# Decay attention with queries on partitions: scores, maximum and exponential on one tile, then transposes

## The chip, the cores and the metric

The kernel runs on one core of a Trainium2 chip. The metric is the device time of one execution in microseconds (us), lower is better. A core has five engines with a queue each, worked off in the order in which the program was written: TensorE (PE, matmuls; its loads of the stationary operand are shown apart as PEld), VectorE (DVE), ScalarE (ACT), GpSimd (POOL) and SyncE (SP, which issues most transfers). Engines wait for one another through semaphores.

## The reference

```
scores = scale * np.matmul(q, k.transpose(0, 1, 3, 2))
log_f = np.log(np.clip(f, 0.0001, 1.0))
cum = np.cumsum(log_f, axis=-1)
decay = cum[:, :, :, None] - cum[:, :, None, :]
scores = np.where(causal, -1000000000.0, scores + decay)
scores = scores - np.max(scores, axis=-1, keepdims=True)
attn = np.exp(scores)
attn = attn / (np.sum(attn, axis=-1, keepdims=True) + 1e-09)
x = np.matmul(attn, v)            # then heads side by side: (B * S, H * D)
h = np.maximum(x @ w_in, 0.0)
out = h * h @ w_out
```

There are 8 batches of 8 heads, that is 64 heads, of S = 576 positions and D = 64 channels. The second part, called the MLP below, has 4608 tokens, 512 channels and 2048 hidden units. All data are float32.

## The kernel before, in words

**Two precisions.** The first NWHOLE = 14 heads ("whole" heads) use float32 operands in the matmuls. All later heads and the MLP ("split" work) write each operand as a high part rounded to float32r plus a low part, and add two or three float32r products.

**Attention, keys on partitions.** For a head, `score` (line 382) makes six units. A unit has up to 128 keys on the partitions and the queries that may see them in the free dimension; the six have 320, 320, 192, 64, 448 and 256 columns, 1600 causal columns in all. Since the maximum of a query runs over partitions there, it is computed earlier and apart: `max_units` (336) makes the product a second time with queries on partitions, and a VectorE instruction (353) adds the causal mask and reduces to the maximum. For whole heads `turn_maxima` (370) turns the maxima into a row by five matmuls with an identity matrix (376); for split heads a transfer writes them as a row (358). The row is an extra contraction row of the score product, as are the two rows of the cumulated decay. So the score product has the maximum subtracted already, and ScalarE takes the exponential from PSUM (408). In split heads GpSimd then zeroes the masked triangle (410), ScalarE makes the high part (423) and VectorE the low part (424). `av_part` (438) multiplies by v: one float32 matmul per piece in whole heads (455), three float32r matmuls in split heads (434 to 436: low x high, high x low, high x high). A column of ones in v gives the denominators; `finish` (472) sends them through DRAM to spread them over the partitions and multiplies (491). Head 7 does the same with matmuls (`finish_here`, 495).

**MLP.** Work is cut into 18 chunks of 256 tokens and 16 slices of 128 hidden units. `mlp1` (548) makes 12 matmuls of 256 columns (554), then ScalarE and VectorE make relu, its square and the split of it (562 to 565). `mlp2` (568), one step behind, makes 6 matmuls of 512 columns (577). A call of either is a "half". The weights arrive as 64-bit floats and are converted by `weight_ops` (185), four VectorE instructions, two on ScalarE and one on GpSimd for each of 32 tiles.

**Order.** Every engine follows the order of the program (`in_order`, 768). The loop at line 739 goes through slots, six for each head. In a slot it issues one score unit, the product with v of the unit two slots earlier (`LAG`), and then whatever the table `events` holds: loads, preparation (`prep`, 304), maxima of the next head. `fill` (662) puts MLP halves into each half of a slot, at the rate at which batches become ready; the MLP can start when batch 0 is done, after eight heads. What is left of the MLP when attention is over (three chunks) runs alone at the end.

**PSUM.** There are eight banks of 512 float32 columns; the table `banks` says which are used for scores (s), maxima (m), the product with v (av), `mlp1` (h) and `mlp2` (o0, o1). It changes when the MLP starts.

## Time and profile before

| | |
|---|---|
| three timed runs | 1221.43, 1227.12, 1228.7 us; median 1227.12 |
| the profiled execution | span 1223.8 us from the first to the last instruction; no other time of its own is given |
| PE busy | 1190.8 us (97%) |
| DVE, ACT, POOL busy | 779.6, 711.3, 371.7 us |
| eight heads without MLP | 0 to 106.2 us |
| attention and MLP together | 106.2 to about 1088 us |
| MLP alone | about 1088 to 1223.8 us |

A row of a timeline has the start, the time from there to the modelled end, the engine, the line, the operation, and the tiles as "written <- read". Since matmuls are pipelined, the distance from one start to the next is what a matmul costs its engine; the duration in the row also has the way through the array. A row of the groups has the summed busy time, the mean of one instruction in ns, and the idle time before it. A row of the windows has for each engine the busy time and the number of instructions, and for PE the granted clock, 1.00 being full speed.

### The profile page before, as it was taken

The page shows a single profiled execution, that of the slowest core. Times are in us where ns is not written, and L with a number is a line of the kernel's source. Part 1 is how long each engine was busy: PE and PEld are TensorE (multiplying, and loading weights), DVE is VectorE, ACT ScalarE, POOL GpSimd, SP SyncE. Part 2 cuts the span into 40 slices and gives each one's busy share as a digit, 9 for nine tenths or more (in the row PEclk, how much of TensorE's full clock was granted, in tenths as well). Part 3 has the DMA queues.
Part 4 walks back from the last instruction along what each step waited for, and adds up shares of the span by engine and source line. Part 5 has one row for each costly group of instructions (what it writes and reads, how often), then busy time and mean ns, then how long its engine had stood idle before and what let it go on. Part 6 is the DMA issues. An engine that isn't in the chain of part 4 may idle for free. (4 is left out here: it accounts for less than half of the span.)

```text
span 1223.8 us, 23339 instructions
## 1 busy us (share of the span) xinstructions
PE 1190.8 (97%) x7808; PEld 1049.1 (86%) x7808; DVE 779.6 (64%) x2049; ACT 711.3 (58%) x1748; POOL 371.7 (30%) x565
## 2 busy tenths in 40 slices
PE   6999998999999999999999999999999999999998
PEld 3666886888998899999999989998999899999997
DVE  5779876666766767675655776667676667533332
ACT  2676665656666666665656566666666666533232
POOL 3333324333334333332322333333333333200000
PEclk7989999999999999999999999999999999999999
DMA  8758500221211212111111111212121212000000
GB/s 234 198 149 237 139 26 17 59 59 39 56 42 40 51 42 58 42 34 41 44 32 43 44 42 42 59 41 54 35 51 37 59 42 59 11 28 11 8 18 18
DMA packets 105912, 71.58 MB, mean 58 GB/s; under 512 B 87848, under 2 KB 87848, under 8 KB 105792
## 3 DMA queue, kind: packets, MB, share of 16 engines
q1 hardware_dynamic: 104672, 65.96, 21.3%
q0 software_dynamic: 1120, 4.13, 1.4%
q8 instruction: 62, 1.02, 0.4%
q14 instruction: 58, 0.48, 0.1%
HBM read 59.91 MB, written 9.87 MB: 57 GB/s over the span
## 5 line engine op out<-in xcount | busy, mean ns | idle before, releaser
L577 PE MATMUL bank<-w,gh 128*128 128x512 f32 x1152 | 414.1, 400 | 0.0
L554 PE MATMUL bank<-xh,w 128*128 128x256 f32 x2304 | 328.5, 285 | 0.2 <-DVE xh L541 0.2
L424 DVE TENSOR_TENSOR pl<-p,ph 128x320 fp32r<-128x320 f32 (+4 forms) x300 | 186.7, 622 | 198.2 <-ACT ph L423 192.1
L554 PEld LDWEIGHTS bank<-xh,w 128*128 128x128 f32 x2304 | 300.6, 189 | 7.8 <-ACT r L562 1.2
L577 PEld LDWEIGHTS bank<-w,gh 128*128 128x128 f32 x1152 | 217.6, 189 | 38.2
L562 ACT ACTIVATE r<-bank 128x256 f32<-128x256 f32 x288 | 110.5, 384 | 208.4 <-PE bank L554 175.9
L577 PE MATMUL bank<-w,gl 128*128 128x512 f32 x576 | 227.2, 394 | 0.1
L563 DVE TENSOR_TENSOR g<-r 128x256 f32<-128x256 f32 x288 | 126.2, 438 | 134.9 <-ACT r L562 134.4
L423 ACT CAST ph<-p 128x320 fp32r<-128x320 f32 (+4 forms) x300 | 124.4, 415 | 150.1 <-POOL p L410 107.6
L410 POOL TENSOR_SCALAR_AFFINE_SELECT p<-p 128x128 f32<-128x128 f32 (+1 forms) x250 | 81.2, 325 | 427.9 <-ACT p L408 321.0
L554 PE MATMUL bank<-xl,w 128*128 128x256 f32 x1152 | 184.2, 282 | 0.0
L353 DVE CUSTOM_DVE_ANT_0 bank<-bank,mz 128x256 f32<-128x256 f32 (+4 forms) x320 | 133.9, 432 | 41.3 <-PE bank L345 39.5
L554 PEld LDWEIGHTS bank<-xl,w 128*128 128x128 f32 x1152 | 157.8, 190 | 0.2 <-DVE xl L542 0.2
L408 ACT ACTIVATE p<-bank 128x320 f32<-128x320 f32 (+4 forms) x300 | 116.3, 388 | 64.0 <-PE bank L401 52.8
L565 DVE TENSOR_TENSOR gl<-g,gh 128x256 fp32r<-128x256 f32 x288 | 127.9, 444 | 35.8 <-ACT p L408 1.0
L345 PE MATMUL bank<-rk 66*128 66x320 f32 (+4 forms) x384 | 112.6, 324 | 18.1 <-DMA rk<-qkraw 10.1
L564 ACT ACTIVATE gh<-r 128x256 fp32r<-128x256 f32 x288 | 120.6, 419 | 9.4
L577 PEld LDWEIGHTS bank<-w,gl 128*128 128x128 f32 x576 | 109.3, 190 | 14.3 <-DVE gl L565 0.9
L434 PE MATMUL bank<-pl,vh 128*65 128x320 f32 (+4 forms) x350 | 97.1, 277 | 2.3 <-ACT den L470 2.3
L345 PEld LDWEIGHTS bank<-rk 66*128 66x128 f32 (+1 forms) x384 | 69.2, 187 | 32.9 <-issue 11.9
L435 PE MATMUL bank<-ph,v 128*64 128x320 f32 (+4 forms) x350 | 94.9, 271 | 0.0
L436 PE MATMUL bank<-ph,vh 128*65 128x320 f32 (+4 forms) x350 | 93.6, 273 | 0.0
(92 smaller groups left out, 1539.5 us busy)
## 6 DMA issues: line engine op xcount, KB each, us to landing
qkraw<-in_qk SPq DMA_DIRECT2D x50, 288.0 KB
v<-in_v SPq DMA_DIRECT2D x64, 160.0 KB
out<-osb SPq DMA_DIRECT2D x36, 256.0 KB
den<-rdr SPq DMA_DIRECT2D x62, 144.0 KB
w<-in_w_in SPq DMA_DIRECT2D x16, 512.0 KB
w<-in_w_out SPq DMA_DIRECT2D x16, 512.0 KB
rl<-in_qk SPq DMA_DIRECT2D x14, 288.0 KB
rk<-in_qk POOLq DMA_DIRECT2D x14, 288.0 KB, 5.5
```

The costliest lines, as they stand in the source:

```text
L345: nc.tensor.matmul(ps[:m, :n], st["r2"][:D + 2, q0:q0 + m], st["kl0"][:D + 2, k0:k0 + n], start=True, stop=True,)
L353: nc.vector.tensor_tensor_reduce(out=ps[:m, :n], in0=ps[:m, :n], in1=mz[:m, mo:mo + n], op0=ALU.add, op1=ALU.min, scale=-1.0, scalar=init, ...
L408: nc.scalar.activation(out=p[:kn, :n], in_=ps[:kn, :n], func=AF.Exp, scale=SCALE)
L423: nc.scalar.copy(out=ph[:kn, :n], in_=p[:kn, :n])
L424: nc.vector.tensor_tensor(out=pl[:kn, :n], in0=p[:kn, :n], in1=ph[:kn, :n].bitcast(F32), op=ALU.subtract,)
L434: nc.tensor.matmul(acc[:D + 1, o], vh, pl[:kn, i], start=first, stop=False)
L554: nc.tensor.matmul(ph[:, :T], w[:, s, cc], x[:, cc, :], start=(cc == 0 and k == 0), stop=(cc == NCC - 1 and k == 2),)
L562: nc.scalar.activation(out=r, in_=ph[:, :T], func=AF.Relu)
L563: nc.vector.tensor_tensor(out=g, in0=r, in1=r, op=ALU.mult)
L564: nc.scalar.activation(out=gh, in_=r, func=AF.Square)
L565: nc.vector.tensor_tensor(out=gl, in0=g, in1=gh.bitcast(F32), op=ALU.subtract)
L577: nc.tensor.matmul(po, g[:, ts], w[:, s], start=(fc == 0 and k == 0), stop=(fc == NF - 1 and k == 2),)
```

## The change

**Layout.** Scores are made with the queries on partitions. The queries of a head are five tiles: tile 0 has 64, tiles 1 to 4 have 128, and tile i sees 64, 192, 320, 448 or 576 keys, again 1600 columns. `unit` does one to two tiles: the score matmuls, a VectorE instruction that adds the mask and reduces to the maximum, and the exponential on ScalarE with the maximum as its bias and the denominator as its accumulated output. `max_units`, `turn_maxima`, the mask matmuls (394), the triangle on GpSimd (410), `finish`, `finish_here`, and their transfers go away.

**Scaling.** `normalize` takes the reciprocals of the five denominators (two VectorE instructions) and scales the five tiles in place on GpSimd, widest first.

**Turning.** `turn` makes 15 PE transposes of 128x128 blocks for a head, in four groups that fill PSUM banks C, D, C, D. ScalarE copies each group to SBUF; in split heads this copy is the high part, and VectorE makes the low part from PSUM.

**Product with v.** `attend`, in five parts, uses [v high | v low] as one stationary operand of 128 columns with the high probabilities and v high with the low ones: two matmuls for each piece in place of three. The two halves of the result lie on different partitions; ScalarE copies one and VectorE adds it.

**Rest.** NWHOLE becomes 10. A weight tile's clamp moves from VectorE to GpSimd. Low and high parts of q and k are placed by transfers (`prep`). Scores get PSUM tiles A and B of two banks each; from the start of the MLP on only A, and the product with v only E. There are two sets of probability tiles up to head 10 and one after it. The slots before head 0 are dropped, and weights are converted at a rate of 1.3 steps per slot.

The diff, cut to its core (new functions as they stand in the changed kernel; of the removed lines, which the listing above shows, only a few):

```diff
-    NWHOLE = 14
+    NWHOLE = 10
+    NDOUBLE = 11
-    banks = {"av": [0, 6], "s": [1, 2, 3], "m": [4, 5, 7], "h": [4], "o0": [6], "o1": [7]}
+    banks = {"s": ["A", "B"], "t": ["C", "D"], "av": ["E", "F"], "h": ["F"], "o": ["B"]}
...
+    probs = [[cpool.tile([P, wide(i)], F32, name=f"p{i}") for i in range(NQ)]]
...
-            nc.vector.tensor_scalar(mag, mag, MAG_LOW, MAG_HIGH, ALU.max, ALU.min)
+                nc.gpsimd.tensor_scalar(mag, mag, MAG_LOW, MAG_HIGH, ALU.max, ALU.min)
...
+    def prep(h, part):
+        st = state[h]
+        if part == 0:
+            st["x"] = wk.tile([P, S], F32R, name="qkr", bufs=1)
+            nc.vector.tensor_copy(out=st["x"], in_=st["raw"])
+            st["r"] = Planes(wk.tile([P, 2 * S], F32R, name="rl"))
+        if part == 1:
+            raw = st["raw"]
+            nc.gpsimd.tensor_tensor(out=raw, in0=raw, in1=st["x"].bitcast(F32), op=ALU.subtract)
...
+            nc.sync.dma_start(out=f32(r.q[:D]), in_=f32(x[:D]))
+            nc.sync.dma_start(out=f32(r.k[D:]), in_=f32(x[D:]))
+            nc.sync.dma_start(out=f32(r.q[D:]), in_=y[:D])
+            nc.sync.dma_start(out=f32(r.k[:D]), in_=y[D:])
...
+            load_cum(h, rounded.k)
+            nc.sync.dma_start(out=f32(rounded.q[:D]), in_=f32(x[:D]))
+            nc.sync.dma_start(out=f32(rounded.k[:D]), in_=f32(x[D:]))
...
+    def score(h, i, ps):
...
+        for k0 in range(0, q0 + m, 512):
+            n = min(q0 + m - k0, 512)
+            o = ps[:mm, k0:k0 + n]
+            qs, ks = slice(q0, q0 + mm), slice(k0, k0 + n)
+            split = h >= NWHOLE
+            nc.tensor.matmul(o, st["q"][:NR, qs], st["k"][:NR, ks], start=True, stop=not split)
+            if split:
+                nc.tensor.matmul(o, st["r"].q[:, qs], st["r"].k[:, ks], start=False, stop=True)
+    UNITS = [[(4, 0)], [(3, 0), (0, 448)], [(2, 512), (1, 832)]]
+    def unit(h, u):
...
+        if u < 2:
+            st["s"] = bank("s")
+        s, tcol = st["s"], st["tcol"]
+        for i, c in UNITS[u]:
+            score(h, i, s[:, c:])
+        for i, c in UNITS[u]:
+            q0, m = QT[i]
+            n = q0 + m
+            x = s[:m, c:c + n]
+            mo = S - n if i else S - P
+            nc.vector.tensor_tensor_reduce(
+                out=x, in0=x, in1=mz[:m, mo:mo + n],
+                op0=ALU.add, op1=ALU.min, scale=-SCALE, scalar=1e30, accum_out=tcol[:m, i:i + 1],
+            )
+        for i, c in UNITS[u]:
+            q0, m = QT[i]
+            n = q0 + m
+            nc.scalar.activation(
+                out=st["p"][i][:m, :n], in_=s[:m, c:c + n], func=AF.Exp,
+                bias=tcol[:m, i:i + 1], scale=-1.0, accum_out=st["den"][:m, i:i + 1],
+            )
+    def normalize(h):
+        st = state[h]
+        rd = wk.tile([P, 8], F32, name="rd")
+        nc.vector.tensor_scalar_add(rd[:, :NQ], st["den"][:, :NQ], EPS)
+        nc.vector.reciprocal(out=rd[:, :NQ], in_=rd[:, :NQ])
+        for i in reversed(range(NQ)):
+            q0, m = QT[i]
+            p = st["p"][i][:m, :q0 + m]
+            nc.gpsimd.tensor_scalar(p, p, rd[:m, i:i + 1], None, ALU.mult)
+    BINS = [
+        [(4, 4, 320), (2, 0, 0), (3, 0, 128), (4, 0, 256)],
+        [(2, 1, 0), (3, 1, 128), (4, 1, 256)],
+        [(2, 2, 0), (3, 2, 128), (4, 2, 256)],
+        [(3, 3, 192), (1, 1, 128), (0, 0, 0), (1, 0, 64), (4, 3, 320)],
+    ]
+    AVS = [
+        [(0, 384, 0, 0), (384, 64, 4, 320)],
+        [(0, 384, 1, 0)],
+        [(64, 320, 2, 64)],
+        [(256, 192, 3, 192)],
+        [(0, 192, 0, 0), (192, 64, 1, 128)],
+    ]
+    PARTS = {3: (192, 384), 4: (0, 192)}
+    def turn(h, b):
+        st = state[h]
+        pt = bank("t")
+        for i, j, c in BINS[b]:
+            nc.tensor.transpose(pt[:, c:c + P], st["p"][i][:, j * P:(j + 1) * P], eye)
...
+            ph = wk.tile([P, 512], F32R, name="ph", bufs=3)
+            pl = wk.tile([P, 512], F32R, name="pl", bufs=3)
+            nc.scalar.copy(out=ph[:, c], in_=pt[:, c])
+            nc.vector.tensor_tensor(
+                out=pl[:, c], in0=pt[:, c], in1=ph[:, c].bitcast(F32), op=ALU.subtract,
+            )
...
+    def attend(h, b):
+        st = state[h]
...
+        t = st["t", min(b, 3)]
+        for k, (c, n, j, o) in enumerate(AVS[b]):
...
+            if h < NWHOLE:
+                nc.tensor.matmul(
+                    acc[:NR, o:o + n], st["vr"][:, j * D:j * D + NR], t[:, c:c + n],
+                    start=first, stop=last,
+                )
+            else:
+                ph, pl = t
+                both = [(P, ph), (D, pl)]
+                for m, x in reversed(both) if last else both:
+                    nc.tensor.matmul(
+                        acc[:m, o:o + n], st["vhl"][:, j, :m], x[:, c:c + n],
+                        start=first and m == P, stop=last and m == P,
+                    )
...
+                low = wk.tile([P, 384], F32, name="low", bufs=1)
+                nc.scalar.copy(out=low[:D, :n], in_=acc[D:, :n])
+                nc.vector.tensor_tensor(out=x, in0=acc[:D, :n], in1=low[:D, :n], op=ALU.add)
...
-                    banks.update(s=[1, 2, 3, 5], m=[], av=[0])
+                    banks.update(s=["A"], av=["E"])
...
+        for u in range(3):
+            at(n0 + u, unit, h, u)
+        at(n0 + 3.5, normalize, h)
+        for b, x in enumerate((4.5, 5, 5.5, 6)):
+            at(n0 + x, turn, h, b)
+        for b, x in enumerate((5.5, 6, 6.5, 7, 7.5)):
+            at(n0 + x, attend, h, b)
...
+            at(n0 - 2 * NU + 4, load_split, h)
+            at(n0 - NU + 0.5, prep, h, 0)
+            at(n0 - NU + 1.5, prep, h, 1)
+            at(n0 - NU + 2, prep, h, 2)
+            at(n0 - NU + 3, prep, h, 3)
...
+    RATE = 1.3
```

The order of instructions, at three places. In a row of PE the moving operand stands ahead of the stationary one; eye is the identity, rl and rk hold q and k, p, xh and xl the probabilities, ph and pl their turned copies, w with gh or gl belongs to `mlp2`, xh or xl with w to `mlp1`.

PE, an early head, no MLP yet. Before, around the end of one head and the start of the next:

```order
L376 MATMUL bank_404<-p 65x128 x4
L376 MATMUL bank_410<-p 65x64
L391 MATMUL bank_416<-rl 128x256
L394 LDWEIGHTS mz
L394 MATMUL bank_416<-p,mz 128x128
L455 MATMUL bank_371<-pl,v 65x64
L391 MATMUL bank_425<-rl 128x320
L455 MATMUL bank_371<-ph,v 65x320
L345 MATMUL bank_433<-rk_80 128x256
L345 MATMUL bank_440<-rk_80 128x320
```

Now, from the head's last scores on:

```order
L312 MATMUL bankB<-rl 128x320
L312 MATMUL bankB<-rl 128x192
L379 MATMUL bankC<-eye,xh_84 128x128 x2
L379 MATMUL bankC<-eye,xl_85 128x128
L379 MATMUL bankC<-eye,xh_84 128x128
L379 MATMUL bankD<-eye,xh_84 128x128
L379 MATMUL bankD<-eye,xl_85 128x128
L379 MATMUL bankD<-eye,xh_84 128x128
```

Before, scores of the next unit, maxima of the next head and the product with v of an earlier unit stand between a score and its use. Now the transposes of a head's probabilities follow right behind its last scores, and no other matmul stands between.

PE, a split head in the middle, MLP running. Before:

```order
L398 MATMUL bank_6961<-rk_80 128x192
L401 MATMUL bank_6961<-rl 128x192
L434 MATMUL bank_6967<-pl,vh_84 65x320
L435 MATMUL bank_6967<-ph,v 64x320
L436 MATMUL bank_6967<-ph,vh_84 65x320
L345 MATMUL bank_6971<-rk_79 128x320
L554 MATMUL bank_6979<-xh_6067,w_223 128x256 x8
L554 MATMUL bank_6979<-xl_6068,w_223 128x256 x4
```

Now, the last of four MLP halves that stand between a head's last scores and its transposes, and the transposes:

```order
L484 MATMUL bankB<-w_565,gh 128x512
L484 MATMUL bankB<-w_565,gl 128x512
L484 MATMUL bankB<-w_565,gh 128x512 x2
L484 MATMUL bankB<-w_565,gl 128x512
L484 MATMUL bankB<-w_565,gh 128x512
L379 MATMUL bankC<-eye,p_83 128x128
L379 MATMUL bankC<-eye,p_81 128x128
L379 MATMUL bankC<-eye,p_82 128x128
L379 MATMUL bankC<-eye,p_83 128x128
```

The halves used to be spread evenly between the six units of a head. Now four of them (in the eight heads of the batch that has to cover three chunks, five) stand in one block ahead of the transposes, and the rest between the groups of transposes and the parts of the product.

VectorE, the same stretch of a split head, now:

```order
L334 ISA bankA,tcol<-bankA,mz 128x192
L334 ISA tcol 128x1
L470 TENSOR_TENSOR g<-r 128x256
L472 TENSOR_TENSOR gl<-g,gh 128x256
L349 TENSOR_SCALAR rd<-den_87 128x5
L350 RECIPROCAL rd<-rd 128x5
L470 TENSOR_TENSOR g<-r 128x256
L472 TENSOR_TENSOR gl<-g,gh 128x256
L390 TENSOR_TENSOR pl<-bankC,ph 128x448
```

The reciprocals (349, 350), for which GpSimd waits before it scales, stand behind the square and split of the MLP step that was issued after the head's last scores; and the low part of the first transposed group stands behind those of one more step.

More of the change, by code (lines that the diff above doesn't have):

```diff
@@ L287, in load_rounded, with load_whole, load_split @@
+    def load_whole(h):
+        x = whole[h % 2]
+        state[h] = dict(q=x.q, k=x.k)
+        nc.sync.dma_start(out=x.raw[:D], in_=qk[h])
         if cum:
             load_cum(h, x.k)
[L290 to L295 removed]
+    def load_split(h):
+        raw = wk.tile([P, S], F32, name="raw", bufs=1)
+        state[h] = dict(raw=raw)
+        for i in range(2):
+            nc.sync.dma_start(out=raw[i * D:(i + 1) * D], in_=qk[h][:, i, :])
@@ L370, in turn_maxima @@
-    def turn_maxima(h):
-        for tiles in (range(1, len(QT)), (0,)):
-            ps = bank("m")
-            q0 = QT[tiles[0]][0]
-            for i in tiles:
-                o, m = QT[i][0] - q0, QT[i][1]
-                nc.tensor.matmul(
-                    ps[:D + 1, o:o + m], cols[h % 2][:, i:i + D + 1], eye_r[:, :m], start=True, stop=True,
-                )
-            n = sum(QT[i][1] for i in tiles)
-            nc.scalar.copy(out=state[h]["whole"].q[D:D + 1, q0:q0 + n], in_=ps[D:D + 1, :n])
@@ L569, in mlp2 @@
         if fc == 0:
-            mst["o", c] = [bank(f"o{t}") for t in range(NTT)]
+            mst["o", c] = bank("o")
         gh, gl = mst.pop(("g", c, fc))
```

451 lines of the change are left out of this document (117 added, 334 removed).

## The prediction

> **What bounds the kernel now.** I read the page first, then the busy time by stage (windows), then PE's timeline in the two stages, then the groups of the other engines.
>
> ```profile
> span 1223.8 us, 23339 instructions
> PE 1190.8 (97%) x7808; PEld 1049.1 (86%) x7808; DVE 779.6 (64%) x2049; ACT 711.3 (58%) x1748; POOL 371.7 (30%) x565
> ```
> ```profile
> 0.00:106.20 106.20, 89.19 (x470) 57.43 (x470) 72.73 (x210) 60.47 (x142) 36.55 (x64) 0.87 0.75 200
> 106.20:1088.00 981.80, 970.26 (x6506) 873.20 (x6507) 665.83 (x1746) 610.56 (x1509) 335.20 (x501) 1.00 0.20 50
> 1088.00:1223.80 135.80, 131.34 (x835) 118.46 (x833) 41.09 (x95) 40.25 (x98) 0.00 (x0) 1.00 0.03 13
> ```
> PE sets the end. From 106.2 us on it is idle for 11.5 of 981.8 us, at full clock; there only PE's own work and new waits count. The first 106.2 us are different: eight heads with no MLP beside them, a mean clock of 0.87, and waits. So two questions decide: does the change take work from PE, and does it make PE wait? PE's price list, from its timeline with the MLP running:
>
> ```profile
> 602.57 0.31 PE L434 MATMUL bank<-pl,vh 128*65 128x320 f32 x1
> 602.72 0.30 PE L435 MATMUL bank<-ph,v 128*64 128x320 f32 x1
> 602.86 0.31 PE L436 MATMUL bank<-ph,vh 128*65 128x320 f32 x1
> 603.01 1.11 PE L554 MATMUL bank<-xh,w 128*128 128x256 f32 x8
> 603.96 0.64 PE L554 MATMUL bank<-xl,w 128*128 128x256 f32 x4
> 604.43 0.40 PE L577 MATMUL bank<-w,gh 128*128 128x512 f32 x1
> ...
> 605.83 0.31 PE L398 MATMUL bank<-rk 67*128 67x320 f32 x1
> ...
> 606.48 0.22 PE L434 MATMUL bank<-pl,vh 128*65 128x128 f32 x1
> ...
> 606.60 0.22 PE L436 MATMUL bank<-ph,vh 128*65 128x128 f32 x1
> 606.66 1.17 PE L554 MATMUL bank<-xh,w 128*128 128x256 f32 x8
> ```
> From start to start, 320 float32r columns cost 0.147 us, 128 cost 0.06; a first MLP half costs 1.42 (603.01 to 604.43), a second 1.40 (to 605.83). A pass over a head's 1600 causal columns, in six or seven pieces, is then about 0.77 us. A result comes some 0.16 us after its matmul has left room for the next (0.31 less 0.147).
>
> ```profile
> 74.94 0.49 PE L376 MATMUL bank<-p 128*65 128x128 f32 x5 [0.81 <-DVE p L353]
> 75.27 0.68 PE L391 MATMUL bank<-rl 67*128 67x256 f32 x2
> ...
> 78.79 1.27 PE L391 MATMUL bank<-rl 67*128 67x320 f32 x2
> 79.85 0.31 PE L394 MATMUL bank<-p,mz 128*128 128x128 bf16 x1
> ...
> 91.76 0.92 PE L391 MATMUL bank<-rl 67*128 67x448 f32 x2
> 92.52 0.22 PE L394 MATMUL bank<-p,mz 128*128 128x128 bf16 x1
> ```
> A float32 matmul runs as two entries; 448 columns cost 0.76 us (91.76 to 92.52), 1.7 ns a column, so a pass in float32 is 2.7 us. At 78.79 the same kind costs twice as much, 1.06 us for 320.
>
> **PE's own work.** A split head had six passes (maximum, two for scores, three with v): 4.6 us. It gets four (two and two): 3.1 us, and 15 transposes. No row shows a transpose. The nearest is L376: four matmuls of 128 columns and one of 64 with an identity, 0.33 us, so 0.07 to 0.08 each. The lower bound is the 0.06 of the 128-column row; the upper is a float32 matmul, 128 x 1.7 = 0.22. I take 0.08, so 1.2 us, and a split head costs 4.3: 0.3 less. A whole head had 2 x 2.7 + 0.77 + 0.4 (L376) + 0.3 (mask matmuls of L394) = 6.9 us and gets 5.4 + 1.2 = 6.6. Four heads go from whole to split, 6.9 to 4.3. Beside the MLP that makes 50 x 0.3 + 4 x 2.6 + 2 x 0.3 = **26 us less**; at 0.06 per transpose 42 less, at 0.22 about 92 more.
>
> The Trainium skill (TensorE: Matmul & The Clock Gate, Part 4) speaks against transposes on PE: it gives 275 ns for one of 128x128 in a kernel's context. Read as cost and not as the way through the array, this would add 0.2 us x 15 x 56 = 164 us. The same page's Terms say that transpose mode is four times faster for float32, which fits the low price. In this trace L376 also shows 0.2 to 0.25 us in duration and 0.07 in cost, so I keep 0.08.
>
> **Eight heads without MLP.** The new order has nothing on PE between a head's last scores and its transposes. The durations on that chain:
>
> ```profile
> L353 DVE CUSTOM_DVE_ANT_0 bank<-bank,mz 128x448 f32<-128x448 f32 x64 | 40.2, 629 | 7.8 <-PE bank L345 7.5
> L353 DVE DVE_READ_ACCUMULATOR2_ANT tcol<- 128x1 f32 x264 | 37.3, 141 | 0.0
> L353 DVE CUSTOM_DVE_ANT_0 bank<-bank,mz 128x320 f32<-128x320 f32 x64 | 32.0, 500 | 6.7 <-PE bank L345 5.5
> L353 DVE CUSTOM_DVE_ANT_0 bank<-bank,mz 128x192 f32<-128x192 f32 x64 | 24.8, 388 | 1.1 <-PE bank L345 1.1
> L235 DVE SCALAR_TENSOR_TENSOR osb<-w,osb 128x512 int32<-128x512 int32 x32 | 26.6, 830 | 0.3
> L239 DVE SCALAR_TENSOR_TENSOR osb<-w,osb 128x512 int32<-128x512 int32 x32 | 23.3, 728 | 0.4
> L483 DVE RECIPROCAL cmp<-cmp 128x9 f32<-128x9 f32 x31 | 6.7, 216 | 1.1
> L482 DVE TENSOR_SCALAR cmp<-cmp 128x9 f32<-128x9 f32 x31 | 6.3, 202 | 0.0
> ```
> ```profile
> L423 ACT CAST ph<-p 128x448 fp32r<-128x448 f32 x50 | 28.3, 567 | 26.1 <-POOL p L410 26.1
> L408 ACT ACTIVATE p<-bank 128x192 f32<-128x192 f32 x50 | 16.5, 331 | 3.7 <-PE bank L401 2.8
> ```
> ```profile
> 600.67 1.43 POOL L491 TENSOR_TENSOR xt<-xt,den 128x576 f32<-128x576 f32 x1
> ...
> 614.02 0.24 POOL L410 TENSOR_SCALAR_AFFINE_SELECT p<-p 66x64 f32<-66x64 f32 x1 [3.27 <-ACT p L408]
> ...
> 618.39 0.29 POOL L410 TENSOR_SCALAR_AFFINE_SELECT p<-p 128x128 f32<-128x128 f32 x1 [2.62 <-DVE tcol L353]
> ```
> The scaling on GpSimd is not in the trace. With one input, like L410, it costs 0.29 + 0.8 ns for each column over 128: 0.65, 0.55 and 0.45 us for the 576, 448 and 320 columns that the first transposes need, 1.65 together. Like the two-input L491 (2.4 ns a column) it would be 3.4. I take 1.65, since it has one tensor input.
>
> Chain: result 0.16, two maxima 0.50 + 0.14 + 0.39 + 0.14, two weight steps that stand ahead of the reciprocals 0.83 + 0.73, reciprocals 0.42 (the exponential, 0.33, is done by then), scaling 1.65: 5.0 us in which PE has nothing. Then four transposes and their result 0.48, copy 0.57, three transposes 0.24, 448 columns with v 0.76, five transposes 0.4, 384 columns 0.65, all five score tiles of the next head 2.7, the other 768 columns with v 1.3. Sum 12.1 us a head at full clock, of which PE works 6.4 after the gap.
>
> ```profile
> 75.00:80.00 5.00, 4.62 (x20) 2.96 (x21) 2.70 (x8) 3.76 (x9) 1.40 (x1) 0.70 1.00 255
> 80.00:85.00 5.00, 5.00 (x21) 3.51 (x20) 2.70 (x11) 2.42 (x7) 1.89 (x3) 0.61 0.18 42
> ```
> Here, after a gap of 0.81 us, the clock was halved for about 6.9 us (2 x 0.30 x 5 + 2 x 0.39 x 5). After gaps of 5 us in every head I expect that often: between 0 and 3.3 us a head, I take 2.2, so 14.3. The Trainium skill (same page, Part 1) has the clock halve after an idle window of 3.4 us and recover after a busy one; by it a head would lose 1.7 and the stage 4 us less. The trace differs, with its short gap and long penalty.
>
> The first score waits for the rows of the cumulated decay as the first maximum did, which ran at 19.05; at half clock five tiles take 5.4 us. The MLP then starts at 24.4 + 8 x 14.3 = 139 us, where it started at 106.2: **33 us more**. Bounds: 12.1 a head gives 15 more, 15.4 gives 41, 10.6 (weight steps off the chain) 3; GpSimd at L491's price adds 14.
>
> **Beside the MLP: is the chain covered?** In 48 of the 56 heads four MLP halves, 5.64 us, stand between the last scores and the transposes.
>
> ```profile
> L562 ACT ACTIVATE r<-bank 128x256 f32<-128x256 f32 x288 | 110.5, 384 | 208.4 <-PE bank L554 175.9 <-DVE pl L424 15.3 <-PE bank L345 9.8
> L564 ACT ACTIVATE gh<-r 128x256 fp32r<-128x256 f32 x288 | 120.6, 419 | 9.4
> L565 DVE TENSOR_TENSOR gl<-g,gh 128x256 fp32r<-128x256 f32 x288 | 127.9, 444 | 35.8 <-ACT p L408 1.0 <-PE bank L394 0.5
> ```
> From the last score: VectorE is free after 0.35 (the sum of the previous head's halves), maxima till 1.5, exponential till 1.85. The reciprocals queue behind the MLP step that PE ends at 1.42: relu till 2.25, square till 2.65, low part till 3.1, reciprocals till 3.5, scaling of three tiles till 5.15. That is 0.5 us before PE comes, so no wait by this sum; with L491's price it ends at 6.9 and PE waits 1.2. The cover gone, 3.5 us more a head would be seen, 170 in all.
>
> VectorE can be held up meanwhile:
>
> ```profile
> 614.78 1.07 DVE L424 TENSOR_TENSOR pl<-p,ph 66x64 fp32r<-66x64 f32 x1
> ```
> This 64-column subtraction took 1.07 us while GpSimd's L323 ran. The new scaling runs back to back for over 2 us a head, with square and low part queued behind it on VectorE, and behind them the low part that frees PSUM bank C; and scores share one PSUM tile, whose release (copy 0.57, low part 0.63, maximum, exponential) takes as long as its cover of 1.92 us. I add 0.35 us for each of 48 heads and 0.2 for the eight with five halves: **18 us more**, bounds 0 and 58 more than that (1.2 each). Until the weights are converted, in heads 10 to 12, VectorE has about 11.7 us of a head's work (maxima 3.2, low parts 2.3, MLP 3.5, the rest 2.7) and 5.9 of conversion, more than PE's 15.6: **5 us more**. What goes away elsewhere (transfers of maxima and denominators, ScalarE's copies of them, GpSimd's triangles and one of its subtractions) was beside PE's work and counts nothing.
>
> **Sum.** 1223.8 + 33 - 26 + 18 + 5 = 1254 in the profiled execution's terms; the median of the runs is 3 above its span: **1257 us**, its own range 1235 to 1285.
>
> **Rivals.**
> - Faster: the first heads run with short gaps (10.6 us a head, 3 more), transposes cost 0.06 (42 less), no new waits: 1188. For it: PE is the bound, and 0.06 is in the trace. Against it: the 5 us hole in each early head.
> - No change: hole at full clock (15 more), 26 less, 5 of waits: 1221. For it: the clock is 1.00 in most of the early windows.
> - Scaling is dear, and PE waits for GpSimd in every head. At 1.6 ns a column, halfway between the two prices, three tiles take 2.4, which gives 0.3 a head beside the MLP (14) and 6 early: 1277; at L491's price the 14 becomes 58 and the 6 becomes 14: 1329. It decides from 2.15 us on for the three tiles.
> - A transpose costs a float32 matmul, 0.22: 118 more beside the MLP, 17 early: 1392. Against it: the L376 rows.
>
> **How the numbers follow.** Chances: forecast 0.50, faster 0.13, no change 0.17, dear scaling 0.15, dear transposes 0.05. A measurement of this kernel tells about 1% from no change. Slower by over 1%: 0.50 + 0.15 + 0.05 = 0.70; within: 0.17; faster: 0.13. The range of 1200 to 1320 takes in the no-change case and most of dear scaling, and leaves out about 0.18.
>
> **What would show it.** The first MLP matmul at about 139 us, PE idle for some 5 us in each early head, with GpSimd's scaling as releaser of the first transposes, and a clock near 0.75 there; transposes 0.06 to 0.08 us apart; waits of PE beside the MLP of some 20 us. I am wrong if the MLP starts before 120 us, if the transposes stand 0.2 us apart, or if the widest scaling takes over 1 us.

## The result: slower by a third, and the profile after

The changed kernel takes 1643.66 us (median of four runs, 1639.70 to 1647.47), the kernel before 1225.63 (four runs, 1221.43 to 1228.70). The ratio is 1.340, with a 95% interval of 1.335 to 1.345. The forecast was 1257 us in a range of 1200 to 1320: the direction was right, the size was not. Of 418 us it had accounted for 30.

The head of the page of the changed kernel answers to the one of before:

```profile
span 1637.9 us, 22389 instructions
PE 1310.3 (80%) x7836; PEld 1117.4 (68%) x7836; DVE 761.5 (46%) x1927; ACT 627.4 (38%) x1704; POOL 580.4 (35%) x524
```

PE was busy for 97% of the span, now for 80%; no other engine took its place. So PE waits. The busy time by stage (cut at the first MLP matmul and at the end of the last attention matmul; columns as before, the third number from the end is the granted clock), first now, then the kernel before:

```profile
0.00:187.40 187.40, 99.17 (x368) 61.07 (x368) 74.38 (x174) 72.11 (x181) 118.27 (x115) 0.68 0.36 119
187.40:1492.60 1305.20, 1073.36 (x6599) 933.27 (x6598) 641.52 (x1651) 512.11 (x1418) 462.10 (x410) 0.94 0.24 62
1492.60:1637.90 145.30, 137.75 (x871) 123.04 (x870) 45.57 (x103) 43.22 (x105) 0.00 (x0) 0.99 0.04 15
```
```profile
0.00:106.20 106.20, 89.19 (x470) 57.43 (x470) 72.73 (x210) 60.47 (x142) 36.55 (x64) 0.87 0.75 200
106.20:1069.70 963.50, 951.96 (x6392) 856.72 (x6393) 657.34 (x1727) 603.55 (x1493) 333.72 (x500) 1.00 0.20 50
1069.70:1223.80 154.10, 149.64 (x948) 134.94 (x947) 49.58 (x114) 47.26 (x115) 1.48 (x1) 1.00 0.05 17
```

Before, PE was idle for 17.0, 11.5 and 4.5 us of the three stages. The early heads thus cost 81 us more and the stage beside the MLP 342 more, 220 of them idle time of PE that was not there before. The tail is 9 shorter: 77 of the MLP's matmuls that ran alone before (948, now 871) now run beside the attention. What PE waits for, over the whole span (us in total, times, longest):

```profile
PE bankC L379 <- POOL p L354: 157.8, 75, 8.2
PE bankA L312 <- ACT p L341: 61.4, 44, 1.5
PE bankC L379 <- POOL xh L354: 37.6, 9, 8.2
PE bankB L484 <- ACT osb L490: 19.3, 18, 1.9
PE bankF L461 <- ACT r L469: 12.9, 12, 1.4
PE bankB L312 <- ACT p L341: 10.0, 5, 2.5
PE bankF L461 <- DVE xh L448: 9.2, 7, 2.5
PE bankB L312 <- ACT xl L341: 7.2, 4, 1.9
```

The first and third row are one wait: a head's first transposes wait for the scaling on GpSimd (xh and xl are the spare memory that holds a second set of probabilities; in rows of L461, the first MLP matmul, xh is the MLP's input). The second is new as well: beside the MLP, scores wait until ScalarE's exponentials have read their PSUM tile. The rows of bankB are the same wait in the early heads, 17.2 us in nine times. The groups of GpSimd, by shape, give the price of the scaling:

```profile
L354 POOL TENSOR_SCALAR p<-p,rd 128x576 f32<-128x576 f32 x59 | 105.1, 1782 | 218.0 <-DVE rd L350 214.6 <-DVE xh L448 3.4
L354 POOL TENSOR_SCALAR p<-p,rd 128x448 f32<-128x448 f32 x59 | 84.7, 1436 | 0.0
L354 POOL TENSOR_SCALAR p<-p,rd 128x320 f32<-128x320 f32 x59 | 64.2, 1088 | 0.0
L354 POOL TENSOR_SCALAR p<-p,rd 128x192 f32<-128x192 f32 x59 | 44.8, 760 | 0.0
L354 POOL TENSOR_SCALAR p<-p,rd 64x64 f32<-64x64 f32 x59 | 25.7, 436 | 0.0
```

That is 4.31 us for the three tiles that the first transposes need (the forecast had 1.65, and its dearest rival 3.4) and 5.50 for all five. One head beside the MLP, from the timeline:

```profile
898.34 0.19 DVE L350 RECIPROCAL rd<-rd 128x5 f32<-128x5 f32 x1
898.63 0.63 PE L461 MATMUL bankF<-xl,w 128*128 128x256 f32 x4
898.70 5.53 POOL L354 TENSOR_SCALAR p<-p,rd 128x576 f32<-128x576 f32 x5 [7.30 <-DVE rd L350]
...
899.76 0.42 DVE L470 TENSOR_TENSOR g<-r 128x256 f32<-128x256 f32 x1 [1.23 <-ACT r L469]
900.32 0.42 DVE L472 TENSOR_TENSOR gl<-g,gh 128x256 fp32r<-128x256 f32 x1
900.48 0.33 PE L379 MATMUL bankC<-eye,p 128*128 128x128 f32 x1 [1.22 <-POOL p L354]
903.13 0.90 PE L379 MATMUL bankC<-eye,p 128*128 128x128 f32 x3 [2.32 <-POOL p L354]
903.68 0.77 PE L484 MATMUL bankB<-w,gh 128*128 128x512 f32 x1
...
904.25 0.63 PE L484 MATMUL bankB<-w,gl 128*128 128x512 f32 x1
```

PE waits 1.22 us for the widest tile and 2.32 for the next two. VectorE's operations at 899.76 and 900.32 run at their usual 0.42 us beside the scaling: what the forecast feared does not happen here. The matmuls after the wait last longer, since the clock is granted at half (0.50 from 903 to 910): the first of 512 columns stands 0.57 us ahead of the next, where six of them otherwise take 1.40.

### The profile page after: what moved, and what is told of

Its sections match the earlier page's. It is cut to its first block, busy times and chain, and to the rows that moved or that the text cites. A ratio compares the mean times of both kernels' runs of the same rounds, so it can differ in the third digit from the quotient of the medians.

```text
span 1637.9 us, 22389 instructions
## 1 busy us (share of the span) xinstructions
PE 1310.3 (80%) x7836; PEld 1117.4 (68%) x7836; DVE 761.5 (46%) x1927; ACT 627.4 (38%) x1704; POOL 580.4 (35%) x524
## 5 line engine op out<-in xcount | busy, mean ns | idle before, releaser
L484 PE MATMUL bankB<-w,gh 128*128 128x512 f32 x1152 | 435.6, 417 | 19.3 <-ACT osb L490 19.3
L354 POOL TENSOR_SCALAR p<-p,rd 128x576 f32<-128x576 f32 x295 | 319.7, 1100 | 218.0 <-DVE rd L350 214.6
L461 PE MATMUL bankF<-xh,w 128*128 128x256 f32 x2304 | 347.8, 296 | 22.1 <-ACT r L469 12.9
L461 PEld LDWEIGHTS bankF<-xh,w 128*128 128x128 f32 x2304 | 317.4, 199 | 38.2 <-ACT r L469 16.1
L470 DVE TENSOR_TENSOR g<-r 128x256 f32<-128x256 f32 x288 | 138.6, 481 | 351.7 <-ACT r L469 351.6
L484 PEld LDWEIGHTS bankB<-w,gh 128*128 128x128 f32 x1152 | 225.4, 196 | 66.9 <-ACT osb L490 28.0
L341 ACT ACTIVATE p<-bankA,tcol 128x576 f32<-128x576 f32 x275 | 143.7, 526 | 295.0 <-DVE tcol L334 290.2
L296 POOL TENSOR_TENSOR vhl<-v,vhl 128x320 fp32r<-128x320 f32 x54 | 47.0, 871 | 591.4 <-PE bankE L413 565.9
L484 PE MATMUL bankB<-w,gl 128*128 128x512 f32 x576 | 232.6, 404 | 1.4 <-DVE gl L472 1.3
L461 PE MATMUL bankF<-xl,w 128*128 128x256 f32 x1152 | 192.2, 291 | 0.7 <-DVE xl L449 0.7
L334 DVE CUSTOM_DVE_ANT_0 bankA<-bankA,mz 128x448 f32<-128x448 f32 (+1 forms) x284 | 142.1, 500 | 69.7 <-PE bankA L312 59.4
L461 PEld LDWEIGHTS bankF<-xl,w 128*128 128x128 f32 x1152 | 166.2, 200 | 1.2 <-DVE xl L449 1.2
```

The source lines that it names most:

```text
L334: nc.vector.tensor_tensor_reduce(out=x, in0=x, in1=mz[:m, mo:mo + n], op0=ALU.add, op1=ALU.min, scale=-SCALE, scalar=1e30, accum_out=tcol[ ...
L341: nc.scalar.activation(out=st["p"][i][:m, :n], in_=s[:m, c:c + n], func=AF.Exp, bias=tcol[:m, i:i + 1], scale=-1.0, accum_out=st["den"][:m ...
L354: nc.gpsimd.tensor_scalar(p, p, rd[:m, i:i + 1], None, ALU.mult)
L461: nc.tensor.matmul(ph[:, :T], w[:, s, cc], x[:, cc, :], start=(cc == 0 and k == 0), stop=(cc == NCC - 1 and k == 2),)
L470: nc.vector.tensor_tensor(out=g, in0=r, in1=r, op=ALU.mult)
L484: nc.tensor.matmul(po, g[:, ts], w[:, s], start=(fc == 0 and k == 0), stop=(fc == NF - 1 and k == 2),)
```

## The experiments

Times are medians of four runs, with the ratio to the kernel before and its interval where that is given; the kernels without the scaling, with the clamp moved, with extra matmuls, with three forms and with doubled transposes ran once each. All waits are PE's.

**What the scaling costs, and where.** In the first kernel the scaling moves to VectorE; in the second it is left out.

```diff
-            nc.gpsimd.tensor_scalar(p, p, rd[:m, i:i + 1], None, ALU.mult)
+            nc.vector.tensor_scalar(p, p, rd[:m, i:i + 1], None, ALU.mult)
```

> The five scalings of normalize move from GpSimd to VectorE, nothing else. Theory A (the price of the scaling on GpSimd, 1.78 + 1.44 + 1.09 us for the three tiles that the first transposes need, is the main cause): on VectorE they take about 1.4 us, the waits of PE for the scaling fall from 195 us to under 40, the first MLP matmul moves from 187 us to 155 to 165, and the time falls to 1400 to 1480 us. Theory B (the order itself, with one score tile and gaps that halve the clock, is the cause, and GpSimd only comes last): the next wait takes the place and the time stays above 1560 us.

> The scaling by the reciprocal denominators is left out (the reciprocals are still computed). This is the floor for any cheaper scaling. Theory A: 1370 to 1440 us, the rest of the loss being the hole of the early heads, the score tile and the clock. Theory B: above 1540 us.

On VectorE: 1435.54 us, 1.171 times the kernel before (1.164 to 1.178). Left out: 1404.02. Both are in theory A's ranges; the waits for the scaling fell from 195 us to 46, where under 40 was expected. The same operation, in VectorE's groups:

```profile
L354 DVE TENSOR_SCALAR p<-p,rd 128x448 f32<-128x448 f32 x59 | 31.2, 529 | 0.0
L354 DVE TENSOR_SCALAR p<-p,rd 128x576 f32<-128x576 f32 x59 | 30.8, 522 | 2.1
L354 DVE TENSOR_SCALAR p<-p,rd 128x320 f32<-128x320 f32 x59 | 23.1, 392 | 0.0
```

1.44 us for the three, a third of GpSimd's price, and 208 us less in the whole. So 240 of the 418 us go with the scaling; 178 are there without it.

**The clamp back to VectorE, and a warmer PE.** The change had also moved a clamp (L191) to GpSimd. One kernel undoes that alone; another issues unused bf16 matmuls (512 columns, 14 in an early head, 5 in a later one) ahead of a head's first transposes.

```diff
-                nc.gpsimd.tensor_scalar(mag, mag, MAG_LOW, MAG_HIGH, ALU.max, ALU.min)
+                nc.vector.tensor_scalar(mag, mag, MAG_LOW, MAG_HIGH, ALU.max, ALU.min)
```
```diff
+        if b == 0:
+            for _ in range(14 if h < 8 else 5):
+                nc.tensor.matmul(pt, mz[:, :P], mz[:, :512], start=True, stop=True)
         for i, j, c in BINS[b]:
```

> The clamp of the weight tiles goes back from GpSimd (2.0 us each, 32 of them) to VectorE (0.5 us each), the scaling stays. If GpSimd as a whole is what the early heads wait for, the first MLP matmul moves from 187 us to 165 or less and the time falls by 20 to 30 us, to about 1615. If only the scaling on its own chain counts, the time stays within 8 us of 1644.

> 14 (first eight heads) or 5 (later) extra bf16 matmuls of 512 columns, results overwritten, run on PE ahead of a head's first transposes, where PE waits for the scaling. If the gaps are what halves the clock, the clock rises from 0.94 to 0.98 or more beside the MLP and the time falls by 50 to 90 us, to 1555 to 1595, though the scaling takes as long as before. If the clock does not follow the gaps, the clock stays at 0.94 and the time is 1640 or more.

The clamp: 1635.19 us, 8 less, and the MLP still starts at 188.3 us (187.4 in the change). So GpSimd's load as a whole is not what the early heads wait for; the chain through the scaling is what counts. The extra matmuls: 1609.31 us, 34 less, between the two expectations. The granted clock beside the MLP rose from 0.94 to 0.97. So part of the loss is the half clock that follows the waits, and these matmuls, which take some 50 us of PE's time beside the MLP, much of it inside the waits, bring back only some of it.

**Which form of the scaling is dear.**

```diff
+            if i == 3:
+                nc.gpsimd.tensor_tensor(out=p, in0=p, in1=rd[:m, i:i + 1].broadcast_to([m, q0 + m]), op=ALU.mult)
+            elif i == 2:
+                nc.gpsimd.tensor_scalar(p, p, 0.5, None, ALU.mult)
+            else:
...
```

> The changed kernel with the scaling still on GpSimd, in three forms: the 448-column tile as a product of two tiles (the reciprocal broadcast over the columns), the 320-column tile by the constant 0.5 (the normalisation of this tile's 128 rows is left out), the others as in the change, by one scalar per partition. Theory: a one-input pass of GpSimd costs some 2.7 ns a column in any form, and only the masking operation of the kernel before was cheaper. Then the constant costs 1.0 to 1.15 us at 320 columns, as the scalar did (1.09), the product 1.4 us or more at 448, and the time stays at 1630 to 1665. Rival: what costs is to read a scalar per partition; then the constant takes 0.45 to 0.6 us at 320 columns, and the time falls by 20 us or more.

```profile
L359 POOL TENSOR_SCALAR p<-p,rd 128x576 f32<-128x576 f32 x59 | 105.2, 1784 | 217.1 <-DVE rd L350 213.7 <-DVE xh L453 3.4
L357 POOL TENSOR_SCALAR p<-p 128x320 f32<-128x320 f32 x59 | 62.3, 1055 | 0.6
L355 POOL TENSOR_TENSOR p<-p,rd 128x448 f32<-128x448 f32 x59 | 56.9, 964 | 0.0
```

A constant costs what the scalar cost (1055 and 1088 ns at 320 columns), so it is not the reading of a scalar. But the product of two inputs costs 964 ns at 448 columns where the scalar form takes 1436: my theory that any form costs this is refuted. The form TENSOR_SCALAR is the dear one. The time was 1595.62, below the range that the theory gave. With all five as products:

> The changed kernel with all five scalings on GpSimd, but as products of two tiles (the reciprocal broadcast), the form that took 0.94 us at 448 columns where the scalar form takes 1.44. Theory: the time follows the price of a head's five scalings: 5.5 us gave 1643.7, 4.9 gave 1595.6, VectorE's 2.0 gave 1435.5 and none 1404. The five products should take 3.3 to 3.8 us, and the time 1480 to 1525. Rival: an operation of GpSimd with two inputs holds up VectorE's (one of 256 columns took 1.59 us beside such a one); then the maxima and splits of VectorE come late too and the time is over 1540.

1546.34 us (1.259, 1.255 to 1.263), above the theory's mark and at the rival's. The five came to 1193, 1188, 895, 567 and 295 ns, 4.1 us and not 3.3 to 3.8; the product of 448 columns took 964 ns in the kernel with three forms and 1188 here, which was not taken apart. VectorE's two operations of an MLP step, 481 and 436 ns on average in the changed kernel, took 527 and 511; over 288 steps that is 35 us on an engine that is not the bound. So GpSimd with two inputs does slow VectorE, slightly, and how much of the 1546 that makes is not separated. In order of the price of a head's five scalings: none 1404.0; 2.0 us 1435.5; 4.1 us 1546.3; 5.0 us 1595.6; 5.5 us 1643.7. The first 2 us cost 16 us each, those after that 52 to 96. That fits a cover that ends there, but does not show it, since engines and forms differ between these kernels.

**The price of a transpose.** Each is issued twice, with the scaling on VectorE.

```diff
-            nc.tensor.transpose(pt[:, c:c + P], st["p"][i][:, j * P:(j + 1) * P], eye)
+            for _ in range(2):
+                nc.tensor.transpose(pt[:, c:c + P], st["p"][i][:, j * P:(j + 1) * P], eye)
```

> Scaling on VectorE (1435.5 us), and every transpose is issued twice, to the same place, so that the second writes what the first wrote. Theory: a transpose costs TensorE its spacing, 0.093 us, as one follows the other in the profile; 840 more beside the MLP cost 78 us and 120 more in the early stage some 11 to 25: 1510 to 1545. Rival 1: each costs what its row shows as its duration, 0.28 us or more: over 1650. Rival 2: they are hidden in TensorE's idle time: below 1470.

1533.95 us, in the theory's range: 98 more for 960 transposes, 0.102 each. The price is the spacing; the 0.28 us that a row shows is the way through the array. The spacing is also read here, from the kernel with the scaling on VectorE:

```profile
749.97 0.71 PE L379 MATMUL bankD<-eye,p 128*128 128x128 f32 x5
750.43 0.42 PE L413 MATMUL bankE<-ph,vhl 128*128 128x384 f32 x1
750.69 0.34 PE L413 MATMUL bankE<-pl,vhl 128*64 128x384 f32 x1
750.87 0.39 PE L312 MATMUL bankA<-rk 66*128 66x512 f32 x1
```

Five transposes take 0.46 us (749.97 to 750.43). The first pass with v after them takes 0.26 for 384 columns, the second 0.18.

**The early heads.** With the scaling on VectorE, the first seven heads' transposes and products stand 2.5 slots later, behind the next head's scores.

```diff
-            at(n0 + x, turn, h, b)
+            at(n0 + x + (2.5 if h < H - 1 else 0), turn, h, b)
...
-            at(n0 + x, attend, h, b)
+            at(n0 + x + (2.5 if h < H - 1 else 0), attend, h, b)
...
-        at(n0 - NU + 2.5 if h else 0, load_v, h)
+        at(n0 - NU + (4.5 if 2 <= h <= H else 2.5) if h else 0, load_v, h)
```

With them, v is loaded two slots later for heads 2 to 8.

> Scaling on VectorE (1435.5 us), and for the first seven heads, which run without MLP work, the transposes and the product with v 2.5 slots later, so that the next head's scores are issued ahead of them. Theory: these heads are late (MLP start at 154.5 us, before 106.2) because each is one chain, scores to exponentials to scaling to transposes, and TensorE's order lets no two heads overlap. Then the MLP starts at 112 to 132, and the time is 1395 to 1417. Rival: an engine's own work sets the early stage (VectorE is busy for 92.6 of its 154.5 us, ScalarE 72.1); then the MLP starts after 145, and the time is 1425 to 1440.

1422.01 us (1.158, 1.155 to 1.162), the MLP starts at 137.1: between the two. The chain of each head is part of it. What takes its place is a wait for ScalarE's copies out of the transposes' bank (26.9 us, 8 times), which are now queued behind the next head's exponentials.

**Where the other waits beside the MLP come from.** The wait for the exponentials of the same PSUM tile (62.7 us in the kernel with the scaling on VectorE) is the largest there:

```profile
PE bankA L312 <- ACT p L341: 62.7, 44, 1.5
PE bankC L379 <- DVE p L354: 26.9, 17, 5.2
PE bankC L379 <- DVE xh L354: 19.0, 9, 5.2
```

Two kernels change what it waits for: one has the third group of scores half a slot later, the other has that group in a bank of the transposes.

```diff
-        for u in range(3):
-            at(n0 + u, unit, h, u)
+        for u, x in enumerate((0, 1, 2.5)):
+            at(n0 + x, unit, h, u)
```
```diff
-    UNITS = [[(4, 0)], [(3, 0), (0, 448)], [(2, 512), (1, 832)]]
+    UNITS = [[(4, 0)], [(3, 0), (0, 448)], [(2, 0), (1, 320)]]
...
-        if u < 2:
-            st["s"] = bank("s")
+        st["s"] = bank("s" if u < 2 else "t")
```

> Scaling on VectorE as in the first experiment (1435.5 us), and a head's third group of scores (query tiles 2 and 1) half a slot later, with half an MLP step between it and the second. Theory: the second largest loss is that these scores wait until the exponentials of the second group, which lie in the same PSUM tile, have been read (62.7 us, 44 waits); a matmul step in between hides it. Then this wait falls below 20 us and the time to 1375 to 1405. Rival: the exponentials, the scaling and the transposes come later by the same, and TensorE waits there instead: the waits of the transposes grow by what these lose, and the time stays within 15 us of 1435.

> Scaling on VectorE (1435.5 us), and the third group of scores written to a PSUM bank of the transposes, which is free then, where the change writes them beside the second group, in the same tile. The order of the work is unchanged. Theory: a wait goes without coming back elsewhere only if what follows comes earlier, not later, as it did with the third group half a slot later (1450.8 us). Then the wait of these scores (62.7 us) falls below 10, no other grows by over 15, and the time is 1355 to 1395. Rival: VectorE's and ScalarE's own order sets when a head's last exponential is done; then the transposes wait instead and the time stays within 15 us of 1435.

> The three edits that help or should: scaling on VectorE, the third group of scores in its own bank, and the next head's scores ahead of the transposes in the first seven heads. Theory: they add up, 1435.5 less 13.5 less what the own bank gives, 1340 to 1385, still slower than before, because TensorE's own work beside the MLP is larger and the early heads remain longer. Rival: the gains overlap or move, and the time is over 1400.

Half a slot later: 1450.76 us (1.182, 1.179 to 1.186); the wait fell to 2.9 us, those of the transposes rose from 45.9 to 75.9, and those for ScalarE's copies of the MLP's output (osb) and for the MLP's inputs (xh) by 32 together. The own bank: 1427.88 (1.163, 1.159 to 1.167), 8 less; that wait went, and another came:

```profile
PE bankF L460 <- ACT r L468: 45.3, 42, 3.0
```

With the early overlap as well 1419.44 (1.156, 1.151 to 1.160), so the rivals held: the times are 15.2 and 7.7 us from 1435.54, the first just past the 15 that its rival allowed, and the third is over 1400. The wait moves, since the chain behind it stays. The timeline of the kernel with the own bank shows that chain:

```profile
679.70 1.42 POOL L276 TENSOR_TENSOR raw<-raw,qkr 128x576 f32<-128x576 f32 x1
...
679.81 1.60 DVE L469 TENSOR_TENSOR g<-r 128x256 f32<-128x256 f32 x1 [1.07 <-ACT r L468]
...
681.48 0.64 PE L460 MATMUL bankF<-xl,w 128*128 128x256 f32 x4
...
682.25 0.48 DVE L333 CUSTOM_DVE_ANT_0 bankC<-bankC,mz 128x320 f32<-128x320 f32 x1
...
683.32 0.53 ACT L340 ACTIVATE p<-bankC,tcol 128x320 f32<-128x320 f32 x1 [2.76 <-DVE tcol L333]
...
684.24 0.38 ACT L468 ACTIVATE r<-bankF 128x256 f32<-128x256 f32 x1
...
684.67 1.22 PE L460 MATMUL bankF<-xh,w 128*128 128x256 f32 x8 [1.15 <-ACT r L468]
```

PE has the MLP's hidden values ready at 682.1, but ScalarE's activation of them (L468) stands behind two exponentials, and these wait for VectorE's maxima. Two causes offer themselves: VectorE is late because GpSimd's two-input operation holds it (1.60 us for what else takes 0.43), or the activation is in the wrong place in ScalarE's queue. First the two subtractions of GpSimd (L276 and L296; the lines below are those of L276) on VectorE, then the exponentials half a slot later in the program, so that they stand behind the activation:

```diff
-            nc.gpsimd.tensor_tensor(out=raw, in0=raw, in1=st["x"].bitcast(F32), op=ALU.subtract)
+            nc.vector.tensor_tensor(out=raw, in0=raw, in1=st["x"].bitcast(F32), op=ALU.subtract)
...
```
```diff
             at(n0 + u, unit, h, u)
+            at(n0 + u + (0.5 if h >= H else 0), exps, h, u)
```

> The kernel of the own bank (1427.9 us), and the two subtractions of a split head's preparation, q and k less their rounded part and v less its own, on VectorE instead of GpSimd. Theory: TensorE's new wait there (45 us, 42 times, for the MLP's activation on ScalarE) begins at GpSimd: its product of two inputs (1.43 us) holds up VectorE (1.60 us for an operation that otherwise takes 0.43), so the maxima, the exponentials and the activation queued behind them are late. On VectorE the two cost some 0.6 and 0.45 us. Then this wait falls below 15 us and the time to 1370 to 1405. Rival: ScalarE's queue is late by its own exponentials, whatever GpSimd does; then the wait stays over 30 us, and the time within 12 us of 1428 or above.

> The same with the next head's scores ahead of the transposes in the first seven heads, so all edits that helped together. Theory: 8 us less than the kernel that has the two subtractions on VectorE and not this, as it was between the two kernels before (1419.4 against 1427.9); so 1360 to 1398, and still slower than the kernel before. Rival: over 1410.

> The kernel of the own bank (1427.9 us), and beside the MLP a group's exponentials half a slot later in the program, so that they stand behind the MLP's activation in ScalarE's queue where an MLP step lies between. Theory: TensorE waits for that activation (45 us, 42 times) only because it is queued behind exponentials that themselves wait for VectorE's maxima; no engine is short of time. Then this wait falls below 20 us, none grows by as much, and the time is 1375 to 1408. Rival: the exponentials are needed at once, and with them later the transposes or the scores wait: the time stays within 12 us of 1428 or grows.

> The same with the next head's scores ahead of the transposes in the first seven heads. Theory: 1365 to 1400, the best of the variants and still slower than before. Rival: over 1412.

The subtractions on VectorE: 1445.03 us (1.175, 1.171 to 1.179), 17 slower, with that wait at 63.3 us, and with the early overlap 1441.13: that theory fell as it stood, though VectorE then has the two operations (0.76 and 0.49 us) to do itself. The exponentials behind the activation: **1351.08** (1.103, 1.101 to 1.105), 77 less and below the range expected, and the wait is down to two short ones:

```profile
PE bankF L465 <- ACT r L473: 1.3, 2, 0.8
```

A stretch of its timeline has the new order: the activation (L473 here) follows PE's matmul, ahead of the exponentials (L345), and PE's next matmul into that bank does not wait:

```profile
483.07 0.64 PE L465 MATMUL bankF<-xl,w 128*128 128x256 f32 x4
...
483.75 0.39 ACT L473 ACTIVATE r<-bankF 128x256 f32<-128x256 f32 x1 [0.67 <-PE bankF L465]
...
484.49 0.51 ACT L345 ACTIVATE p<-bankD,tcol 128x320 f32<-128x320 f32 x1
...
484.93 1.12 PE L465 MATMUL bankF<-xh,w 128*128 128x256 f32 x8
```

No engine has fewer operations to do than in the kernel with the own bank; only ScalarE's order differs. VectorE is even busy for longer beside the MLP (744 us for 720, with the same 1931 instructions), since more of its operations now run beside GpSimd's subtractions, and the wait is gone all the same; so that hold alone is not what cost the time. With the early overlap it is 1341.69 (1.096, 1.093 to 1.098), again below the range expected and the best version found: 302 us faster than the change, and still 10% slower than the kernel before.

**The scaling again, with the order mended.**

> The kernel with the own bank and the exponentials behind the activation (1351.1 us), with the scaling back on GpSimd as in the change. Theory: the scaling's price (5.5 us a head there, 2.0 on VectorE) costs its own, whatever the order: MLP start at 180 to 190, some 2.5 us a head beside the MLP, 1525 to 1570. Rival: beside the MLP most of the 208 us that it cost in the change was the order of ScalarE's queue; then only the early heads lose (some 33 us), and the time is below 1430.

> The best variant (1341.7 us) with the scaling left out (the probabilities stay unnormalised). Theory: VectorE's five scalings are then worth the early heads' chain alone: MLP start at 120 to 128, 1318 to 1335, and what is left over the kernel before, some 100 us, is TensorE's own work (transposes 78 us) and the early heads. Rival: the scaling still costs beside the MLP; below 1310.

Back on GpSimd: 1568.82 us (1.279, 1.273 to 1.284), 218 more than 1351.08, with the MLP's start at 176.8 us and so earlier than expected. The scaling's price hardly depends on the order: it cost 208 in the change. Left out of the best version: 1328.07 in one run, 14 less, but not where it was expected: the MLP starts at 138.6 us, 3 later than with the scaling, and the gain is beside the MLP.

## Why the prediction was wrong

By stage, in us from the profiled executions; "own bank" and "order" are the kernels with the third group's bank and with the exponentials behind the activation, "best" has the early overlap as well:

| | span | early heads | beside the MLP | PE idle there | tail |
|---|---|---|---|---|---|
| before | 1223.8 | 106.2 | 963.5 | 11.5 | 154.1 |
| the change | 1637.9 | 187.4 | 1305.2 | 231.8 | 145.3 |
| no scaling | 1402.2 | 138.8 | 1118.1 | 108.2 | 145.3 |
| scaling on VectorE | 1433.0 | 154.5 | 1130.6 | 117.0 | 147.9 |
| with own bank | 1425.2 | 150.8 | 1129.2 | 102.0 | 145.2 |
| with own bank and order | 1351.7 | 151.1 | 1055.3 | 52.0 | 145.2 |
| best | 1334.2 | 135.2 | 1053.7 | 54.1 | 145.3 |
| best, no scaling | 1326.3 | 138.6 | 1042.4 | 43.8 | 145.3 |

1. **The step that failed first: the scaling's price.** "I take 1.65, since it has one tensor input": it is 4.31. The row chosen for it, the affine select of L410, was the wrong neighbour, and L491, two inputs and 3.4, was no upper bound: in this case the scalar form of GpSimd costs more than its product of two tiles. The prediction named the point from which the price decides (2.15 us) and what would show it wrong ("if the widest scaling takes over 1 us"; it takes 1.78). It is worth 236 us here (1637.9 less 1402.2): 49 in the early heads, 187 beside the MLP. Even with 4.31 in its own sum the forecast would have been too low: 4.31 less the 2.15 of cover, in 48 heads, is 104, and 2.66 more in eight early heads is 21; that makes some 1380.

2. **What that sum lacked: the clock.** With and without the scaling PE executes the same 6599 matmuls beside the MLP; they take 1073.4 us and 1009.9, at a mean granted clock of 0.94 and 0.98. The row without the scaling:

```profile
138.80:1256.90 1118.10, 1009.91 (x6599) 897.49 (x6598) 636.55 (x1651) 511.69 (x1418) 159.39 (x130) 0.98 0.28 72
```

By the trace's records of the clock, PE was busy at half clock for 125 us with the scaling and for 36 without; half of the difference, 44 of the 63 us, is what the clock cost. The other 19 were not taken apart. The forecast had counted the clock in the early heads alone, where it had seen that one gap of 0.81 us halves it for 6.9 us.

3. **"18 us more" for new waits beside the MLP.** Without any scaling PE's idle time still rose by 97. The forecast looked for the cause in VectorE, held up by GpSimd, and in the scores' shared PSUM tile. Neither was enough: the tile's wait moved when the tile was split, and VectorE was held up more, not less, in the kernel that lost the wait. The exponentials stood ahead of the MLP's activation in ScalarE's queue and waited there for the maxima; 77 us went when the two changed places, in the kernel with the own bank; how much of that the own bank is needed for was not run. The chain of this term was summed engine by engine, and no line asked what is queued behind an instruction that waits.

4. **"26 us less" of PE's own work.** It is 25 more, the attention's matmuls beside the MLP taken from each start to the next (to the end where a gap follows), in the kernel with the scaling on VectorE. As foreseen, 46 us of passes for the maxima went, and 3 for masks and for turning the maxima. The transposes cost 82 and not 67, at 0.093 for 0.08 and some at the end of a wait. The scores cost 6 more. The products with v fell by 14 us, where one of three passes should have taken about 43 with it: one part is in the rows at 750.43, where the first pass after transposes stands 0.26 us ahead of the next and not 0.18; the rest was not taken apart.

5. **"33 us more" for the early heads.** 81, and 33 with no scaling at all. So the forecast's 14.3 us a head were reached without the 1.65 of scaling that they contained, and that the two agree is luck. Its chain had all five score tiles run without a stop; but the third group waits for the exponentials of the second, which lie in the same PSUM tile (bankB, 17.2 us in nine times, the same without the scaling). It also lacked ScalarE's readings of the accumulated sums and the longer exponentials (below). The mechanism, a hole between scores and transposes at a lower clock (0.68), is the one foreseen; with GpSimd's price a head takes 20.4.

6. **What held.** PE's work and its waits set the time; the first transposes wait for GpSimd; a transpose costs its spacing. The reading of the Trainium skill's 275 ns (TensorE: Matmul & The Clock Gate, Part 4) as the way through the array and not as cost agrees with this case: rows of 0.28 us and more, and 0.102 us in the time for each.

What stays open: the best version without scaling is 102 us above the kernel before in span. 32 of that are the early heads and 9 come back in the tail; beside the MLP it is 79. Of these, 32 are idle time of PE, where the longest waits left are those for ScalarE's copies of the MLP's output (18) and for the MLP's inputs (13); 13 are the attention's matmuls, counted as under 4; and 34 are the MLP's matmuls, some 12 of them for the 77 that stood in the tail before. The remaining 21 or so weren't taken apart; a granted clock below 1.00 (15 us lost in PE's busy time, 2 before) is part of what is left.

## What to carry to other kernels

Price an operation on an engine by a row of the same form of instruction on that engine; a neighbour with fewer or more inputs is no bound, and where none exists the price decides the range. For every instruction that will wait, list what stands behind it in its queue: here the exponentials, harmless by their own 2.6 us a head from start to start, held up the MLP's activation, and moving them half a slot was worth 77 us. A wait that goes from one place to another when its target is removed (1435, 1451, 1428) has its cause further up the chain; look for the queue in which the order can be changed.

## What the runs showed of the hardware

- GpSimd's TENSOR_SCALAR in float32 costs 0.25 us and 2.66 ns a column, with a scalar per partition, and as much with a constant where that was run (1055 ns at 320 columns); a product with the reciprocal broadcast 0.96 to 1.19 us at 448 columns, for 1.44, and 1.19 at 576, for 1.78; with two whole tiles of 576 columns it took 1.45 (L276). The affine select of the kernel before took 0.345 us at 128 columns. VectorE does the same scaling of 576 columns in 0.52 us, GpSimd in 1.78. The Trainium skill (GPSIMD Engine Reference, section 4.1, Engine selection) has GpSimd about half as fast as VectorE with two inputs and roughly at the line rate with one; for the scalar form this case disagrees, by 3.4 times. That the durations hold is seen on another engine: of the five that run from 898.70 on, the first should be done at 900.48 and the third at 903.01, and PE's transposes that wait for them start at 900.48 and 903.13.
- While GpSimd ran the scalar form, VectorE's two-input operations kept their 0.42 us (0.44 on average for the 55 squares that it overlapped most); while it subtracted two tiles of 576 columns, one of them took 1.60 us instead of 0.43.
- An exponential that also accumulates its sum is followed by a reading of 0.19 us on ScalarE, and its row is 0.1 us longer (634 ns at 448 columns, 531 in the kernel before). The rows overlap: to the next instruction the two take 0.52 us at 320 columns, where the exponential alone took 0.33 before. Two of the rows, from the kernel after:

```profile
L341 ACT ACTIVATION_READ_ACCUMULATOR p<-bankA,tcol 128x1 f32 x221 | 43.0, 194 | 0.0
L341 ACT ACTIVATE p<-bankA,tcol 128x448 f32<-128x448 f32 x54 | 34.2, 634 | 89.6 <-DVE tcol L334 84.7 <-PE bankF L461 4.8
```
